# Attention into a two-layer MLP on one core: loads and weights in a new order, the fifth unit's attention outputs beside the output product, DVE's normalising tiles first

## The chip, the cores and the metric

The kernel runs on one core of one Trainium2 chip. The metric is the device time of one execution in microseconds (us); smaller is better. The engines of the core work side by side and wait for each other by semaphores: PE (TensorE, matrix products, with PEld for its weight loads), ACT (ScalarE), DVE (VectorE), POOL (GpSimd) and SP (SyncE, which here only issues DMAs).

## The reference, cut to what matters

```python
# q, k, v: (8 batches, 12 heads, 448 rows, 64), times 0.1
scores = matmul(q, k.T) / sqrt(64)
m = max(scores, axis=-1)
e = exp(scores - m)
attn = e / (sum(e, axis=-1) + exp(-m) + 1e-9)
x = concat_heads(matmul(attn, v))          # (8 * 448, 768)
h = x @ w_in                               # w_in  (768, 2048)
g = h * tanh(softplus(h))                  # Mish
out = g @ w_out                            # w_out (2048, 768)
```

Inputs and output are float32; the kernel casts to bfloat16 for its matrix products.

## The kernel before, in words

**Pairs and units.** Two heads are a pair: 48 pairs, p = 0 to 47, six to a batch. Three pairs are a unit u; two units are a batch. The first six pairs (u = 0 and 1) run in a loop of their own, the head. From u = 2 on, one iteration of the main loop does two parts. The attention part has twelve steps, n = 0 to 11, four for each of the unit's three pairs. The matrix part, f = 0 to 7, multiplies the attention output of the batch two units back by an eighth of `w_in` at a time. The third to sixth unit of the title are u = 2 to 5, and the fifth is u = 4.

**A step of attention.** `scores` writes one score tile (PE) and takes its row maxima (DVE, line 293). There are three score tiles of two banks each, and `scores_ahead` keeps up to three filled. `exps` takes the exponentials on ACT (line 306); after it the tile is free. Of a pair's four steps three have two column blocks, and one has one block and leaves its second bank unused.

**Normalising.** `normalise(p)` multiplies the seven column blocks of a pair's exponentials (the buffer `en`) by the reciprocal denominators `rden`. In the head POOL does four (`shared=4`) and DVE three (lines 339 and 341); POOL reads its own copy of the reciprocals (line 331). In later units DVE does two pairs and POOL the third (`on_pool`). The result is turned either by a DMA transpose on SP's queue (line 345) into `eT`, or on PE by `turn_on_pe` (line 356) for the pairs in `BY_PE` (2, 4, 5, 6, 7).

**Attention output.** `av_pair` does eight matmuls (line 382) from `eT` and `v_bf` and copies the result into `xT` (line 391). It writes either one of the two product tiles `mo` (`mo_take`), or, where `bank` is given, the unused second bank of a pair's last score tile. The main loop uses the second way for all units from u = 4 on, through `av_with`. For u = 2 and 3 the list `AV_AT` says after which step which pair's output is made in a product tile.

**The products.** `mm1_mish` does the first product and Mish (lines 406 and 412). `mm2_part` does the second (line 472) for 128 rows and a number of quarters of the 768 columns; `plan` says which parts belong to which unit. A part is cut into chunks of two matmuls, which the attention steps take in between as filler, by `weight`. `gather_mid` copies 64 rows of each of two batches into one tile, used by the part with i = 3. Copies out of the product tiles are put off (`late`) until the next `flush_late`.

**Loads.** `load_pair` issues the three loads of a pair (224 KB each) on SP's queue, where the DMA transposes and the stores of the output stand too, each in the order of the program. `cast_pair` casts them on POOL. In the main loop both happen at the steps n = 0, 3 and 6 (`LOAD_AT`): loads four pairs ahead, casts three. `load_w` issues the twenty pieces of the weights (twelve of `w_in` with 256 KB, eight of `w_out` with 384 KB) on POOL's queue, by `W_HEAD` in the head and by `W_AT` from u = 2 to 4, with two more at f = 2 and 6 of u = 2.

What the engines do is in the order of the program; there is no scheduler behind it (`manual_schedule`).

Of the kernel before, what the change touches and what calls it, by code (L numbers as in the profile page):

```python
# [9 lines left out]
FP32 = mybir.dt.float32  # L10
BF16 = mybir.dt.bfloat16
AF = mybir.ActivationFunctionType
ALU = mybir.AluOpType
# [6 lines left out]
def kernel(  # L20
# [9 lines left out]
    nc = tc.nc  # L30
# [6 lines left out]
    SP_ = S // NT  # L37
# [3 lines left out]
    NTILE = 2 * S // 128  # L41
    UNITS_PER_B = HP // UNIT_PAIRS
# [10 lines left out]
    def pool(name, bufs, space=None):  # L53
        if space is None:
            return ctx.enter_context(tc.tile_pool(name=name, bufs=bufs))
        return ctx.enter_context(tc.tile_pool(name=name, bufs=bufs, space=space))
# [6 lines left out]
    st_pool = pool("st", 5)  # L63
# [48 lines left out]
    def flush_late():  # L112
        while late:
            late.popleft()()
# [8 lines left out]
    def load_pair(p, which="qkv"):  # L123
        if p >= N_PAIRS:
            return
        b, h0 = p // HP, (p % HP) * 2
        tiles = loaded.setdefault(p, [])
        for nm, src in (("q", q), ("k", k), ("v", v)):
            if nm not in which:
                continue  # L130
            t = ld_pool.tile([SP_, 2, NT * D], FP32, tag=f"{nm}_f", name=f"{nm}_f")
            nc.sync.dma_start(
                out=t, in_=src[b, h0 : h0 + 2].rearrange("h (p t) d -> p h (t d)", t=NT)
            )
            tiles.append(t)
# [19 lines left out]
    def load_w(n):  # L155
        for _ in range(min(n, len(pieces))):
            dst, src = pieces.popleft()
            nc.gpsimd.dma_start(out=dst, in_=src.rearrange("(a p) c -> p a c", p=128))
# [80 lines left out]
    def scores_ahead(limit):  # L239

        while rg["next"] < limit and rg["used"] < len(sc_tiles):
            rg["used"] += 1
            scores(rg["next"])
            rg["next"] += 1
# [80 lines left out]
    def normalise(p, dma=True, on_pool=False, shared=0):  # L325
        st = att[p]
        en = st["en"]
        if on_pool or shared:

            st["rden2"] = st_pool.tile([128, NTILE], FP32, tag="rden2", name="rden2")  # L330
            nc.vector.tensor_copy(out=st["rden2"], in_=st["rden"])  # L331
        for i in range(NTILE):
            pool_does = on_pool or i < shared
            args = dict(
                out=en[:, :, i, 0:SP_], in0=en[:, :, i, 0:SP_],
                scalar1=st["rden2" if pool_does else "rden"][:, i : i + 1],
            )
            if pool_does:
                nc.gpsimd.tensor_scalar(scalar2=1.0, op0=ALU.mult, op1=ALU.mult, **args)  # L339
            else:  # L340
                nc.vector.tensor_scalar(scalar2=None, op0=ALU.mult, **args)  # L341
        eT = eT_pool.tile([128, NT, 2 * S], BF16, tag="eT", name="eT")
        st["eT"] = eT
        if dma:
            nc.sync.dma_start_transpose(
                out=eT.rearrange("c j (i q) -> c (j i) q", q=128),
                in_=en.rearrange("q j i c -> q (j i c)"),
            )
# [64 lines left out]
        if not spare:  # L413
            mo_free.append(h_ps)

    def gather_mid(b):

        g, half = divmod(b, 2)
        if half == 0:
            mids[g] = mid_pool.tile([128, FF_T, 128], BF16, tag="mid", name="mid")  # L420
        at = S - 64 if half == 0 else 0
        nc.vector.tensor_copy(
            out=mids[g][:, :, 64 * half : 64 * half + 64], in_=gT[b][:, :, at : at + 64]
        )

# [59 lines left out]
    first_mm2 = 2 * UNITS_PER_B  # L485

    def whole(g, i):
        return [(g, i, 0, 2), (g, i, 2, 2)]
# [3 lines left out]
    plan = {}  # L492
    for g in range(B // 2):
        u0 = first_mm2 + 4 * g
        rest = plan.pop(u0, [])
        if g == 0:
            plan[u0] = [(0, i, 0, 2) for i in range(2)] + [(0, 2, 0, 1)]
            plan[u0 + 1] = [(0, 2, 1, 1)] + [(0, i, 2, 2) for i in range(3)]
        else:
            plan[u0] = rest + whole(g, 0) + [(g, 1, 0, 1)]  # L500
            plan[u0 + 1] = [(g, 1, 1, 1), (g, 1, 2, 2)] + whole(g, 2)
        plan[u0 + 2] = [(g, 4, 0, 2), (g, 4, 2, 1)] + whole(g, 3)
        plan[u0 + 3] = [(g, 4, 3, 1)] + whole(g, 5) + [(g, 6, 0, 2)]
        if g < B // 2 - 1:
            plan[u0 + 4] = [(g, 6, 2, 2)]
        else:
            plan[u0 + 3] += [(g, 6, 2, 1), (g, 6, 3, 1)]
# [4 lines left out]
    BY_POOL = 4  # L512
    LEAD = UNIT_PAIRS + 1
    LOAD_AT = (0, 3, 6)
    LAST_AV_AT = (0, 6, 9)
    HEAD = HP

# [9 lines left out]
    }  # L527
    AV_HEAD = {(3, 3): 0, (4, 2): 2, (4, 3): 1}
    W_HEAD = {0: 3, 1: 1, 3: 1, 4: 1}
    AV_AT = ({3: 4, 7: 3, 9: 5}, {5: 6, 8: 7, 10: 8})  # L530

    W_AT = ({5: 1, 9: 1}, {1: 1, 4: 1, 5: 1, 7: 1, 9: 1, 11: 1}, {3: 1, 5: 1, 7: 1, 9: 1})
    for which in ("qk", "v"):
        for p in range(UNIT_PAIRS):
            load_pair(p, which)
# [39 lines left out]
    for u in range(UNITS_PER_B, N_UNITS + 2 * UNITS_PER_B):  # L575
        attn = u < N_UNITS
        filler = deque()
        for part in plan.get(u, []):
            filler.extend(mm2_part(*part))
        total, done, acc = sum(w for _, w in filler), 0, 0.0  # L580
        p0 = u * UNIT_PAIRS
        if attn and u >= first_mm2:
            av_with.update({p0 + i: p0 + i - UNIT_PAIRS for i in range(UNIT_PAIRS)})
        end = min((u + 1) * UNIT_PAIRS, N_PAIRS) * STEPS

        for n in range(steps):
            pi, s = divmod(n, STEPS)
            p, idx = p0 + pi, p0 * STEPS + n
            late_tp = u == UNITS_PER_B and n == STEPS
            if late_tp:  # L590
                transpose_pair(p0 + 2)
            exps(idx)
            if late_tp:
                evac_qk(p0 + 2)
            if u == UNITS_PER_B + 1:
                for part in TURN_AT[1].get(n, []):
                    turn_on_pe(*part)
            flush_late()
            acc += weight[n]
            want = int(total * acc / sum(weight) + 1e-6)  # L600
            while done < want:
                fn, w = filler.popleft()
                fn()
                done += w
            scores_ahead(end)
            if n in LOAD_AT:
                load_pair(p0 + LOAD_AT.index(n) + LEAD)
                cast_pair(p0 + LOAD_AT.index(n) + LEAD - 1)
            if u - UNITS_PER_B < len(AV_AT):
                early = AV_AT[u - UNITS_PER_B]  # L610
                if n in early:
                    av_pair(early[n])
                if u == UNITS_PER_B:
                    for part in TURN_AT[0].get(n, []):
                        turn_on_pe(*part)
            elif u == N_UNITS and n in LAST_AV_AT:
                av_pair(p0 - UNIT_PAIRS + LAST_AV_AT.index(n))
            if u - UNITS_PER_B < len(W_AT):
                load_w(W_AT[u - UNITS_PER_B].get(n, 0))
        assert done == total  # L620

        moe = u < N_UNITS + UNITS_PER_B
        b, w = (u - UNITS_PER_B) // UNITS_PER_B, u % UNITS_PER_B
        nxt = p0 + UNIT_PAIRS
        todo = sorted(range(p0, nxt), key=lambda p: p in BY_PE)
        for f in range(FF_U):
            if moe:
                mm1_mish(b, w * FF_U + f)
            if u == UNITS_PER_B and f in (2, 6):
                load_w(1)  # L630
            if not attn:
                continue
            if f == 0:
                denominators(att[p0]["whole"])
                normalise(todo[0], dma=todo[0] not in BY_PE)
            if f in (1, 3, 5):
                transpose_pair(nxt + f // 2, bank=f // 2 % 2)
                evac_qk(nxt + f // 2)
            if nxt < DIAG_FROM and f in (4, 6):
                scores_ahead(nxt * STEPS + f // 2 - 1)  # L640
            if f == FF_U - 1:
                scores_ahead(min(nxt * STEPS + 3, N_PAIRS * STEPS))
            if f == 3:
                normalise(todo[1], dma=todo[1] not in BY_PE)
            if f == 4:
                normalise(todo[2], dma=todo[2] not in BY_PE, on_pool=True)
        if attn and u + 1 < N_UNITS:

            nc.scalar.activation(out=one, in_=zero, func=AF.Exp)
        if moe and w == UNITS_PER_B - 1:  # L650
            gather_mid(b)
    flush_late()
    assert not pieces and all(have == 4 for _, have in o_sbs.values())
# [30 lines left out]
```

## Time and profile before

| | us |
|---|---|
| median of 3 runs | 480.37 (480.23 to 481.23) |
| profiled execution, its own time | 479.95 |
| its span, first to last instruction | 478.0 |
| busy: PE | 443.1 (93%) |
| busy: ACT | 350.0 (73%) |
| busy: DVE | 339.1 (71%) |
| busy: POOL | 181.1 (38%) |
| moved by DMA | 90.37 MB, mean 189 GB/s |

The mean granted clock of PE was 0.982. In the lines of the profile, a row of a timeline has the start and the duration in us, the engine, the line of the kernel, the operation with output and inputs, the count of instructions that were merged into the row, and in brackets the idle time of the engine before it and what ended that. A row of the chain of waits has start, duration and what was being done. `SPq` is the queue of DMAs that SP issues. Slices are fortieths of the span, 11.95 us each.

### The profile page before, as it was taken

Reading aid. Unit: us, or ns where it says so; the run is one execution under the profiler, and the core shown is the slowest. Engines: PE = TensorE matmul, PEld = TensorE weight load, DVE = VectorE, ACT = ScalarE, POOL = GpSimd, SP = SyncE. Lnnn points to the kernel's source line nnn. Section 1 sums busy time; section 2 is a strip of 40 time slices with the busy share of each in tenths; the row PEclk is TensorE's granted clock in tenths of the full one; section 3 lists DMA queues with packets and bytes.
Section 4 is the critical chain, followed back from the end, with each engine's and each line's share of the span. In section 5 each row is a group of like instructions: output and inputs, shape, how many; then the busy total and the mean of one; then the engine's idle time right before and its main releaser. Section 6 shows DMA issues by size and latency. Waiting matters only on the chain.

```text
span 478.0 us, 8924 instructions
## 1 busy us (share of the span) xinstructions
PE 443.1 (93%) x3064; PEld 248.6 (52%) x3064; DVE 339.1 (71%) x680; ACT 350.0 (73%) x919; POOL 181.1 (38%) x315
## 2 busy tenths in 40 slices
PE   4565888898999999999999999999999999999997
PEld 2233544454655555555555555556555555556565
DVE  4888987968787886878687878788787869420021
ACT  5979678878787888979787878888897978412300
POOL 4877809255514334353535242433535340300000
PEclk9998798899999999999999999999999999999999
DMA  8999969999999989899999999899989595870113
GB/s 228 220 233 220 235 100 234 162 187 238 207 217 276 206 212 219 213 203 246 193 250 182 225 167 228 211 207 234 201 233 212 156 178 127 135 164 24 43 28 105
DMA packets 202381, 90.37 MB, mean 189 GB/s; under 512 B 159072, under 2 KB 198880, under 8 KB 202336
## 3 DMA queue, kind: packets, MB, share of 16 engines
q1 hardware_dynamic: 194848, 83.51, 81.3%
q0 software_dynamic: 7488, 6.29, 8.6%
q8 instruction: 24, 0.39, 0.3%
q14 instruction: 21, 0.17, 0.1%
HBM read 45.61 MB, written 11.01 MB: 118 GB/s over the span
## 4 chain that ended last, share of the span: by engine, by line
PE 76%; ACT 10%; DVE 9%; issue 2%; DMA 1%; POOL 0%; SPq 0%; DVEq 0%; ACTq 0%; POOLq 0%
PE mo L472 26%; PE mo L406 25%; ACT en L306 9%; PE sc L382 6%; DVE negm L293 6%; PE sc L266 5%; PE sc L406 4%; PE sc L193 3%; PE sc L272 2%; PE mo L356 1%; PE mo L382 1%; DVE en L341 1%; PE sc L280 1%; DVE eT L360 1%; DMA k_f<-in_k_dram 1%
## 5 line engine op out<-in xcount | busy, mean ns | idle before, releaser
L306 ACT ACTIVATE en<-sc,negm 128x448 bf16<-128x448 f32 x336 | 209.6, 637 | 26.4 <-DVE xT L391 10.4
L293 DVE TENSOR_REDUCE negm<-sc 128x2 f32<-128x896 f32 x192 | 180.7, 968 | 55.8 <-PE sc L275 26.0
L472 PE MATMUL mo<-w_out_sb,gT 128*128 128x384 bf16 (+1 forms) x912 | 142.3, 301 | 0.0
L406 PE MATMUL mo<-xT,w_in_sb 128*128 128x448 bf16 x672 | 137.7, 353 | 0.6 <-DVE xT L391 0.6
L412 ACT ACTIVATE gT<-mo 128x448 bf16<-128x448 f32 x112 | 61.3, 547 | 68.2 <-PE mo L406 68.1
L472 PEld LDWEIGHTS <-gT 128*128 128x128 bf16 x912 | 84.1, 98 | 48.2 <-issue 5.7
L339 POOL TENSOR_SCALAR en<-en,rden 128x448 bf16<-128x448 bf16 x122 | 76.4, 646 | 80.7 <-DVE rden L331 76.9
L406 PEld LDWEIGHTS <-w_in_sb 128*128 128x128 bf16 x768 | 72.9, 98 | 64.0 <-issue 3.0
L306 ACT ACTIVATION_READ_ACCUMULATOR en<-sc,negm 128x1 f32 x336 | 69.3, 206 | 0.0
L175 POOL CAST q_bf<-q_f 112x512 bf16<-112x512 f32 x47 | 29.0, 617 | 98.4 <-DMA q_f<-in_q_dram 98.0
L341 DVE TENSOR_SCALAR en<-en,rden 128x448 bf16<-128x448 bf16 x214 | 58.6, 345 | 0.9
L459 DVE COPY o_sb<-mo 128x384 f32<-128x384 f32 (+1 forms) x65 | 32.2, 495 | 35.1 <-PE mo L472 34.8
L266 PE MATMUL sc<-kT,qd 128*128 128x448 bf16 x168 | 47.7, 354 | 0.3 <-ACT en L306 0.2
L272 PE MATMUL sc<-kT,qd 64*128 64x448 bf16 x72 | 25.1, 411 | 12.7 <-ACT en L306 11.1
L382 PE MATMUL sc<-eT,v_bf 112*64 112x448 bf16 x288 | 34.1, 357 | 1.9 <-ACT en L306 1.7
L162 POOL CAST v_bf<-v_f 112x512 bf16<-112x512 f32 x48 | 29.5, 616 | 9.7 <-DMA v_f<-in_v_dram 8.8
L382 PEld LDWEIGHTS <-v_bf 112*64 112x64 bf16 x384 | 21.0, 112 | 22.8 <-issue 13.6
L176 POOL CAST k_bf<-k_f 112x512 bf16<-112x512 f32 x47 | 28.9, 616 | 7.5 <-DMA k_f<-in_k_dram 7.0
L227 DVE TENSOR_SCALAR qd<-sc 64x448 bf16<-64x448 bf16 x48 | 18.7, 389 | 11.9 <-PE sc L193 11.2
L266 PEld LDWEIGHTS <-qd 128*128 128x128 bf16 x168 | 16.3, 97 | 18.0 <-issue 9.2
L275 PE MATMUL sc<-kT,qd 64*128 64x448 bf16 x72 | 25.4, 415 | 0.0
L472 PE MATMUL mo<-w_out_sb,mid 128*128 128x384 bf16 x128 | 24.9, 326 | 0.0
(57 smaller groups left out, 340.1 us busy)
## 6 DMA issues: line engine op xcount, KB each, us to landing
q_f<-in_q_dram SPq DMA_DIRECT2D x48, 224.0 KB, 5.1
k_f<-in_k_dram SPq DMA_DIRECT2D x48, 224.0 KB, 5.4
v_f<-in_v_dram SPq DMA_DIRECT2D x48, 224.0 KB, 5.7
w_in_sb<-in_moe_w_in_dram POOLq DMA_DIRECT2D x12, 256.0 KB, 6.1
w_out_sb<-in_moe_w_out_dram POOLq DMA_DIRECT2D x8, 384.0 KB, 7.6
out_dram<-o_sb SPq DMA_DIRECT2D x7, 336.0 KB, 3.3
out_dram<-o_sb SPq DMA_DIRECT2D x8, 288.0 KB, 4.6
out_dram<-o_sb SPq DMA_DIRECT2D x8, 240.0 KB, 2.9
```

What stands on the lines that cost most here:

```text
L162: nc.gpsimd.tensor_copy(out=casted[p][2], in_=loaded.pop(p)[2])
L266: nc.tensor.matmul(sc[:, bk, 0:S], lhsT=qT[:, i].rearrange("d h r -> d (h r)"), rhs=kT, start=True, stop=True,)
L272: nc.tensor.matmul(sc[:, 0, 0:S], lhsT=qT[0:64, qa : qa + 128], rhs=kA, start=True, stop=True)
L293: nc.vector.tensor_reduce(out=negm, in_=sc[:, 0 : len(cols), 0:S], axis=AX.X, op=ALU.max, negate=True)
L306: nc.scalar.activation(out=st["en"][:, :, c, 0:SP_], in_=sc[:, bk, 0:S].rearrange("q (j c) -> q j c", j=NT), func=AF.Exp, bias=st["negm"][ ...
L339: nc.gpsimd.tensor_scalar(scalar2=1.0, op0=ALU.mult, op1=ALU.mult, **args)
L341: nc.vector.tensor_scalar(scalar2=None, op0=ALU.mult, **args)
L382: nc.tensor.matmul(av[h * 64 : (h + 1) * 64, 0:S], lhsT=v_bf[:, h, j * D : (j + 1) * D], rhs=e_h, start=(j == 0), stop=(j == NT - 1),)
L406: nc.tensor.matmul(h_ps[:, 0:S], lhsT=w_in_sb[:, dm, ff * 128 : (ff + 1) * 128], rhs=xT[b][:, dm, :], start=(dm == 0), stop=(dm == DM_T - 1),)
L412: nc.scalar.activation(out=gT[b][:, ff, :], in_=h_ps[:, 0:S], func=AF.Mish)
L459: nc.vector.tensor_copy(out=o_sb[:, cols], in_=st["o"][:, 0:n_cols])
L472: nc.tensor.matmul(st["o"][:, 0:n_cols], lhsT=src[:, ff, c0 : c0 + 128], rhs=w_out_sb[:, ff, cols], start=(ff == 0), stop=(ff == FF_T - 1),)
```

## The change

Four things are changed.

- `normalise`: DVE's tiles are issued first, then the copy of the reciprocals, then POOL's tiles. Before, the copy came first and POOL's tiles stood ahead of DVE's in the program.
- The loads of u = 2 to 4 follow a table: pair 13 is loaded at n = 9 and pair 14 at f = 1 of u = 2; pair 15 at n = 0 and pair 16 at f = 5 of u = 3; pair 17 at n = 0 and pair 18 at f = 1 of u = 4. Casts stay where they were. The weight pieces of u = 2 to 4 move by some steps: both of the matrix part of u = 2 at f = 2; in u = 3 one from n = 11 to n = 2; in u = 4 two each at n = 1 and n = 4, before one each at 3, 5, 7 and 9.
- In u = 4 the attention outputs of pairs 9, 10 and 11 are made in product tiles after the steps 2, 7 and 9, and no more in the score tiles. The copy of `gather_mid(0)` moves from DVE, at the end of u = 3, to POOL, after step 7 of u = 4.
- The second product has six quarters in u = 4 and six in u = 5, before five and seven; the part of 128 rows that was cut into two single quarters stays whole.

```diff
     def normalise(p, dma=True, on_pool=False, shared=0):
         st = att[p]
         en = st["en"]
-        if on_pool or shared:
-
-            st["rden2"] = st_pool.tile([128, NTILE], FP32, tag="rden2", name="rden2")
-            nc.vector.tensor_copy(out=st["rden2"], in_=st["rden"])
-        for i in range(NTILE):
-            pool_does = on_pool or i < shared
-            args = dict(
-                out=en[:, :, i, 0:SP_], in0=en[:, :, i, 0:SP_],
-                scalar1=st["rden2" if pool_does else "rden"][:, i : i + 1],
-            )
-            if pool_does:
-                nc.gpsimd.tensor_scalar(scalar2=1.0, op0=ALU.mult, op1=ALU.mult, **args)
-            else:
-                nc.vector.tensor_scalar(scalar2=None, op0=ALU.mult, **args)
+        n_pool = NTILE if on_pool else shared
+
+        def scaled(i, rden):
+            tile_i = en[:, :, i, 0:SP_]
+            return dict(out=tile_i, in0=tile_i, scalar1=rden[:, i : i + 1])
+
+        for i in range(n_pool, NTILE):
+            nc.vector.tensor_scalar(scalar2=None, op0=ALU.mult, **scaled(i, st["rden"]))
+        if n_pool:
+
+            rden2 = st_pool.tile([128, NTILE], FP32, tag="rden2", name="rden2")
+            nc.vector.tensor_copy(out=rden2, in_=st["rden"])
+            for i in range(n_pool):
+                nc.gpsimd.tensor_scalar(
+                    scalar2=1.0, op0=ALU.mult, op1=ALU.mult, **scaled(i, rden2)
+                )
...
-    def gather_mid(b):
+    def gather_mid(b, copy=nc.vector.tensor_copy):
...
-        nc.vector.tensor_copy(
+        copy(
...
         if g == 0:
-            plan[u0] = [(0, i, 0, 2) for i in range(2)] + [(0, 2, 0, 1)]
-            plan[u0 + 1] = [(0, 2, 1, 1)] + [(0, i, 2, 2) for i in range(3)]
+            plan[u0] = [(0, i, 0, 2) for i in range(3)]
+            plan[u0 + 1] = [(0, i, 2, 2) for i in range(3)]
...
+    LOADS = {
+        2: ({0: 10, 3: 11, 6: 12, 9: 13}, {1: 14}),
+        3: ({0: 15}, {5: 16}),
+        4: ({0: 17}, {1: 18}),
+    }
...
-    AV_AT = ({3: 4, 7: 3, 9: 5}, {5: 6, 8: 7, 10: 8})
-
-    W_AT = ({5: 1, 9: 1}, {1: 1, 4: 1, 5: 1, 7: 1, 9: 1, 11: 1}, {3: 1, 5: 1, 7: 1, 9: 1})
+    AV_AT = ({3: 4, 7: 3, 9: 5}, {5: 6, 8: 7, 10: 8}, {2: 9, 7: 10, 9: 11})
+
+    W_AT = ({5: 1, 9: 1}, {1: 1, 2: 1, 4: 1, 5: 1, 7: 1, 9: 1}, {1: 2, 4: 2})
...
-        if attn and u >= first_mm2:
+        if attn and u > first_mm2:
             av_with.update({p0 + i: p0 + i - UNIT_PAIRS for i in range(UNIT_PAIRS)})
...
+            if u in LOADS:
+                if n in LOADS[u][0]:
+                    load_pair(LOADS[u][0][n])
+            elif n in LOAD_AT:
+                load_pair(p0 + LOAD_AT.index(n) + LEAD)
             if n in LOAD_AT:
-                load_pair(p0 + LOAD_AT.index(n) + LEAD)
                 cast_pair(p0 + LOAD_AT.index(n) + LEAD - 1)
...
+            if (u, n) == (first_mm2, 7):
+                gather_mid(0, nc.gpsimd.tensor_copy)
...
-            if u == UNITS_PER_B and f in (2, 6):
-                load_w(1)
+            if u == UNITS_PER_B and f == 2:
+                load_w(2)
+            if u in LOADS and f in LOADS[u][1]:
+                load_pair(LOADS[u][1][f])
...
-        if moe and w == UNITS_PER_B - 1:
+        if moe and w == UNITS_PER_B - 1 and b > 0:
             gather_mid(b)
```

## The prediction

> **What bounds the kernel now.** I read the page's slices first, then the chain of waits, then the timelines of the engines over the stretch that the diff touches (0 to 160 us).
>
> ```profile
> PE   4565888898999999999999999999999999999997
> PEclk9998798899999999999999999999999999999999
> DMA  8999969999999989899999999899989595870113
> ```
>
> TensorE (PE) is full from the tenth slice on, so whatever the early units win or lose is carried to the end unchanged. The DMA engines are nearly full too, with a hole only in the sixth slice (60 to 72 us). A unit from u=6 on lasts 26.0 us (154.84 to 180.83). Unit u=4 lasts 25.9 (102.2 to 128.1), u=5 26.7 (128.1 to 154.84). The PE timeline of these two:
>
> ```profile
> 105.67 0.95 PE L382 MATMUL sc<-eT,v_bf 112*64 112x448 bf16 x8 [0.32 <-ACT en L306]
> ...
> 111.06 0.95 PE L382 MATMUL sc<-eT,v_bf 112*64 112x448 bf16 x8 [0.83 <-ACT en L306]
> ...
> 115.99 0.95 PE L382 MATMUL sc<-eT,v_bf 112*64 112x448 bf16 x8 [0.52 <-ACT en L306]
> ...
> 117.73 1.30 PE L406 MATMUL mo<-xT,w_in_sb 128*128 128x448 bf16 x6
> ...
> 143.81 1.30 PE L406 MATMUL mo<-xT,w_in_sb 128*128 128x448 bf16 x6
> ...
> 149.41 0.36 PE L193 MATMUL sc<-ident,q_bf 112*128 112x112 bf16 x4 [0.51 <-DVE qd L214]
> ```
>
> In u=4 PE idles before each attention output (L382), since that writes a score tile which ACT's exponentials must first leave; with 0.21 at 114.44 that is 1.88 us. Its attention part lasts 14.84 (102.89 to 117.73) with five output quarters, that of u=5 15.04 (128.77 to 143.81) with seven and no idle time. ACT and DVE there:
>
> ```profile
> 109.67 0.63 ACT L306 ACTIVATE en<-sc,negm 128x448 bf16<-128x448 f32 x1 [0.68 <-DVE negm L293]
> ```
>
> ```profile
> 17.36 0.82 DVE L341 TENSOR_SCALAR en<-en,rden 128x448 bf16<-128x448 bf16 x3
> ...
> 28.85 1.13 DVE L341 TENSOR_SCALAR en<-en,rden 128x448 bf16<-128x448 bf16 x3
> ...
> 108.55 3.08 DVE L293 TENSOR_REDUCE negm<-sc 128x2 f32<-128x896 f32 x3
> ...
> 120.00 1.81 DVE L341 TENSOR_SCALAR en<-en,rden 128x448 bf16<-128x448 bf16 x7
> ...
> 146.09 2.97 DVE L341 TENSOR_SCALAR en<-en,rden 128x448 bf16<-128x448 bf16 x7
> ```
>
> DVE's seven normalising tiles take 1.81 us alone and 2.97 at 146.09, where POOL casts; in the head three take 0.82 or, beside POOL's four, 1.13. POOL:
>
> ```profile
> 29.11 2.60 POOL L339 TENSOR_SCALAR en<-en,rden 128x448 bf16<-128x448 bf16 x4 [1.47 <-DVE rden L331]
> ...
> 146.66 0.73 POOL L175 CAST q_bf<-q_f 112x512 bf16<-112x512 f32 x1 [2.40 <-DMA q_f<-in_q_dram]
> ```
>
> The head, in the chain of waits and in ACT's timeline:
>
> ```profile
> 31.45 0.98 PE mo L356 x7
> ...
> 33.85 1.11 PE mo L382 x8
> ```
>
> ```profile
> 35.01 0.53 ACT L391 CAST xT<-mo 128x448 bf16<-128x448 f32 x1 [2.21 <-PE mo L382]
> ```
>
> PE turns pair 2's seven tiles right behind POOL, then does pair 0's attention output, and ACT idles 2.21 us for it: this stretch sets the pace. SP's queue:
>
> ```profile
> 95.03 13.69 SPq L345 DMA_TRANSPOSE eT<-en  x3
> ...
> 121.87 16.58 SPq L345 DMA_TRANSPOSE eT<-en  x3
> ...
> 138.50 0.57 SPq L132 DMA_DIRECT2D q_f<-in_q_dram  x1
> ```
>
> A DMA transpose (0.92 MB) holds SP for 4.3 us alone; u=4's three took 7.2, 4.2 and 4.9, the first beside the last weight pieces (issued until 119.8). All loads of u=5 wait behind them.
>
> **The change part by part**, against the profiled execution's 479.95 (span 478.0 and 1.95 around it; 0.42 under the median 480.37).
>
> *DVE's tiles first* (head, pairs 0 to 5). POOL now starts behind DVE's three tiles: 0.82 less the 0.08 that the copy of the reciprocals took in the queue, +0.74. Its four tiles then run alone: 0.62 each as in the rows of seven (4.33), 2.50 for 2.60. POOL ends 0.64 later; its casts follow, with a pair's slack. Pair 2: PE reaches POOL's fourth tile at 31.39 + 3 x 0.13 = 31.78, POOL ended at 31.71 and will end at 32.35: +0.57, straight into ACT's 2.21. Pair 4 (POOL 43.84 + 2.60, PE at 46.30): fourth tile at 46.69, POOL at 47.08, +0.39, of which the 0.19 between PE's end (47.29) and DVE's pick-up (47.48) is free: +0.20. Pair 5's tiles are on DVE's own chain at 49.83: 1.13 becomes 0.82, -0.31. Pairs 0, 1, 3 go by DMA and are used many us later (20.48 for 33.78): nothing. Sum **+0.46**; bounds -0.31 (POOL never waited for) and +0.96.
>
> *Attention outputs of pairs 9 to 11 in u=4.* They leave the score tiles for the two product tiles, behind steps 2, 7 and 9. Each product tile is free by then (its copy ran a step earlier), and their eT landed by 111 (104.5 + 6.2). Eight matmuls stay eight, but PE no longer waits for ACT before them and the single-column reduction no longer stands behind 0.95 us of them. The copies of xT move too: DVE's reduction of 108.55 was late behind one and an output copy, ACT's idle 0.68. PE without its idle time: 14.84 - 1.88 = 12.96, plus a sixth quarter (8 x 0.163 = 1.31): 14.27. Following steps with ACT at 0.61 per exponential leaves about 0.1: 14.4, **-0.45**. Bounds -0.57 and +0.5 (an output copy of 0.55 waited for).
>
> *Six quarters in u=5.* A quarter less on PE (-1.31) meets ACT: u=4 with five quarters and this form of attention output took 14.84. Here the first output copy is made before the fourth score tile and not between two reductions (0.46 less on DVE). Followed step by step it comes to 14.5, by the row of u=4 to 14.84; I take 14.64, nearer to the first, **-0.40**; bounds -0.1 and -1.31. Two 192-wide halves become one 384-wide: 32 x 0.082 against 16 x 0.163, nothing.
>
> *gather_mid(0) on POOL.* DVE loses 0.78 at 105.63, where it then idled 0.60 for PE: nothing there. POOL's 1024 elements are not in the trace; by casts of 512 at 0.56 apart, 1.1 us, from 0.78 (DVE's) to 1.4 (0.62 per 448). Its user is in u=6; behind it on POOL wait only the copies of q_rest (122.17), idle until then for DVE. What it collides with is a rival.
>
> *Loads and weights.* Load 13 goes into the DMA hole, 14 and 15 two us earlier: their casts (77 to 83 us) never waited, so nothing. Third-unit weight piece ten: 60 us for 76.5, used at 97, nothing. In u=4 weight pieces 16 and 17 go out at 106 and not 115, 18 and 19 behind cast 16 (which waits for its load), by 118. First use of them is at once in u=5, 128.7 for 132.2; a piece lands in 7.6, so 126. POOL's queue behind cast 16 holds only cast 17 and the copy. On SP load 18 stands between u=4's first and second transpose: 1.5 us of issue and up to 3.0 of DMA (0.67 MB at 220 GB/s). The first transpose should fall from 7.2 to 4.4, so the second starts at 128.1 against 129.2 and, sharing the DMA, lands near 136; its attention output comes at 136.3. Third: lands 140.6 for 141.4. I put **+0.20**, bounds 0 and +2.1.
>
> *u=5's matrix part.* It lasted 11.03 (143.81 to 154.84) against 10.37 in u=4: 0.66 lost where cast 20 (load late, behind the transposes) ran into DVE's tiles. SP now stores the first output tile before load 19, load 20 leaves at about 140.8 (141.1 before) and lands at 146, DVE's tiles start at 145.4 (146.09): they overlap for 1.1 us, not 2.0. **-0.40**; bounds 0 and -0.66.
>
> Sum: +0.46 - 0.45 - 0.40 - 0.40 + 0.20 = **-0.59**: 479.36 for the profiled execution, **479.8** for the median.
>
> **The rivals.** 0.2% is 0.96 us, about what a measurement of this kernel can tell from no change: faster is under 479.4, slower over 481.3.
>
> *POOL's later start is not felt* (ACT or the turning PE has slack that the rows hide): the head gives -0.31 and not +0.46, the rest holds, 0.77 less: 479.0. For it: PE's seven turned tiles took 1.05 against 0.99 elsewhere, so POOL was only just felt. Against: PE ran without a gap from 30.90 to 35. Chance 0.24.
>
> *The late second transpose* (slower). If the first transpose still takes 7.2, it ends at 129.1, load 18 at 130.6, the second transpose at 136.3 and lands at 138.4, against 136.3 wanted: PE waits 2.1, ACT behind it. No gain in u=5's matrix part: 480.37 + 0.46 - 0.45 - 0.40 + 2.1 = 482.1. It decides once the first transpose ends after 127. For it: DMA is at 200 to 215 GB/s from 118 to 126. Against: half of those weights go 9 us earlier. Chance 0.18.
>
> *ACT bounds both units*: u=4 gains 0.2, u=5 0.1, the collision stays: 480.37 + 0.46 - 0.30 = 480.5. For it: 21 exponentials and two table loads are most of 15 us; against: the 1.4 us that ACT idles in u=4. Chance 0.12.
>
> *The copy on POOL meets DVE's tiles in u=4* (cast 17 and the copy, 118.9 to 121.7, on DVE's 119.5). At the measured 1.16 per 2.03 us of casts, 2.3 us of POOL cost DVE 1.3; PE's slack there was 0.56 (122.11 to 122.67) and grows by 0.5: +0.3, 480.1; if DVE waits out all of POOL's time, +1.3, 481.1. Chance 0.10. The Trainium skill (SBUF — State Buffer, section "SBUF: two separate sides") says that the pair of ports which DVE's fast modes share with GpSimd is held for a whole instruction and the other side fully blocks. By that rule the higher of the two prices holds; the 2.97 us agree in direction, but 1.16 is less than the casts' whole time.
>
> **How the numbers follow.** Forecast 0.36, its own range 479.2 to 480.4. Faster: 0.23 of the first rival and 0.13 of the forecast, 0.36. Slower: 0.17 of the late transpose and 0.03 of the copy's tail, 0.20. The rest, 0.44, lies within. The range from 478.6 to 481.6 leaves out both gains at their bounds and the upper part of the late transpose.
>
> **What would show it.** Head: POOL's tiles start 0.7 later, three DVE tiles take 0.8, ACT's idle before the first xT copy grows from 2.21 to 2.8. u=4: no idle before L382, attention part 14.4. u=5: 14.6, and its normalising tiles under 2.97. First transpose of u=4 near 4.4. I am wrong if the matrix part of u=4 starts no earlier relative to its table load, if L382 in u=5 waits for a DMA, or if the head does not shift.

## The result and the profile after

The changed kernel takes 483.27 us in the median (482.89 to 483.73) against 480.3 for the kernel before beside it: ratio 1.0062, 95% interval 1.0039 to 1.0086, so 3.0 us slower (1.9 to 4.1). The forecast was 479.8, with a range up to 481.6. The profiled execution spans 481.9 us, 3.9 more than that of before, at the same mean granted clock of 0.982.

The slices of the page:

```profile
PE   4576798799889999999999999999999999999997
PEclk9998798999989999999999999999999999999999
DMA  8999999899999989899999999898989695770103
```

The hole of the DMA engines in the sixth slice is filled, as meant. But PE now has 8s in the eleventh and twelfth slices (120 to 145 us), and the granted clock an 8 in the twelfth, where all were 9 before. I cut the run at the starts of the matrix parts and took each length in both traces. The head is 0.64 longer, u=3 0.87 shorter (before, the granted clock was 0.50 there from 89 to 92; no other kernel's trace here has such a stretch at that place), u=4's attention part 0.54 longer (15.45 to 15.99 between two matrix parts), u=4's matrix part 1.65 longer (10.43 to 12.08), u=5's attention part 2.58 longer (15.65 to 18.23) and u=5's matrix part 0.67 shorter (11.10 to 10.43). From u=6 on the two are equal. The sum is +3.87.

PE's timeline, with the waits of u=4 and u=5 in the brackets:

```profile
106.64 0.54 PE L266 MATMUL sc<-kT,qd 128*128 128x448 bf16 x2 [0.39 <-DVE negm L293]
...
113.05 0.54 PE L266 MATMUL sc<-kT,qd 128*128 128x448 bf16 x2 [0.43 <-ACT en L306]
...
118.04 1.30 PE L408 MATMUL mo<-xT,w_in_sb 128*128 128x448 bf16 x6 [0.29 <-DVE xT L393]
...
124.62 0.36 PE L193 MATMUL sc<-ident,q_bf 112*128 112x112 bf16 x4 [1.48 <-DVE qd L214]
...
140.09 1.43 PE L384 MATMUL sc<-eT,v_bf 112*64 112x448 bf16 x8 [2.02 <-DMA eT<-en]
```

The first three are u=4's attention part: no wait before an attention output (L382 before, L384 now), but other waits in their place. The fourth is in u=4's matrix part and new. The fifth is pair 13's output in u=5; after this wait the granted clock falls to 0.61 and 0.54 for two stretches of 2 us, and the eight matmuls take 1.43 for 0.95. An attention output of u=5 that waits for a DMA is one of the signs that the prediction names for being wrong.

DVE's seven normalising tiles in u=4, first the row of the timeline and then the answer for that line (minimum, median and maximum of one tile in ns), and in u=5:

```profile
118.90 5.37 DVE L335 TENSOR_SCALAR en<-en,rden 128x448 bf16<-128x448 bf16 x7
...
150.63 2.29 DVE L335 TENSOR_SCALAR en<-en,rden 128x448 bf16<-128x448 bf16 x7
```

```profile
L335 DVE TENSOR_SCALAR en<-en,rden x7: 322/681/2220, 118.9 to 123.9; 128x448 bf16<-128x448 bf16 x7
```

Before, the seven of u=4 took 1.81. What POOL did then:

```profile
105.80 1.55 POOL L158 DMA_DIRECT2D w_out_sb<-in_moe_w_out_dram  x2
116.26 0.61 POOL L175 CAST q_bf<-q_f 112x512 bf16<-112x512 f32 x1 [8.91 <-DMA q_f<-in_q_dram]
...
118.84 0.61 POOL L162 CAST v_bf<-v_f 112x512 bf16<-112x512 f32 x1 [0.39 <-DMA v_f<-in_v_dram]
119.39 1.48 POOL L158 DMA_DIRECT2D w_out_sb<-in_moe_w_out_dram  x2
120.86 0.63 POOL L175 CAST q_bf<-q_f 112x512 bf16<-112x512 f32 x1
...
122.61 1.03 POOL L424 COPY mid<-gT 128x1024 bf16<-128x1024 bf16 x1
```

POOL waits 8.91 us for load 16 (5.93 before), and then everything behind it comes in one block from 118.84 to 123.64: the last cast of pair 16, two weight pieces, pair 17, the copy. DVE's tiles, 118.90 to 124.27, run beside that block from its start to its end. SP's queue:

```profile
124.34 4.98 SPq L347 DMA_TRANSPOSE eT<-en  x1
...
131.06 10.52 SPq L347 DMA_TRANSPOSE eT<-en  x2
```

The first transpose of u=4 needs those tiles. It is shorter than before (4.98 for 7.2) but starts 2.5 us later; load 18 follows, and the second transpose starts at 131.06, where the forecast had 128.1. PE's wait of 2.02 is for that one.

### The profile page after: what moved, and what is told of

The parts are those of the page before. It is cut to its first block, busy times and chain, and to the rows that moved or that the text cites. A ratio compares the mean times of both kernels' runs of the same rounds, so it can differ in the third digit from the quotient of the medians.

```text
span 481.9 us, 8886 instructions
## 1 busy us (share of the span) xinstructions
PE 445.6 (92%) x3048; PEld 247.8 (51%) x3048; DVE 341.1 (71%) x678; ACT 349.3 (72%) x919; POOL 180.7 (37%) x316
## 4 chain that ended last, share of the span: by engine, by line
PE 77%; DVE 9%; ACT 7%; DMA 4%; issue 2%; SPq 1%; POOL 1%; DVEq 0%; ACTq 0%; POOLq 0%
PE mo L408 26%; PE mo L474 26%; PE sc L384 6%; ACT en L306 6%; PE sc L266 6%; DVE negm L293 5%; PE sc L408 4%; PE sc L193 3%; PE sc L272 2%; DMA eT<-en 2%; PE mo L384 2%; DVE eT L362 1%; DMA q_f<-in_q_dram 1%; DVE en L335 1%; PE mo L358 1%
## 5 line engine op out<-in xcount | busy, mean ns | idle before, releaser
L474 PEld LDWEIGHTS <-gT 128*128 128x128 bf16 x896 | 82.9, 98 | 50.2 <-issue 7.8
L341 POOL TENSOR_SCALAR en<-en,rden 128x448 bf16<-128x448 bf16 x122 | 75.3, 635 | 79.1 <-DVE rden L339 70.8
L335 DVE TENSOR_SCALAR en<-en,rden 128x448 bf16<-128x448 bf16 x214 | 60.5, 353 | 1.1
L384 PE MATMUL sc<-eT,v_bf 112*64 112x448 bf16 x264 | 31.7, 361 | 2.5 <-DMA eT<-en 2.0
L384 PEld LDWEIGHTS <-v_bf 112*64 112x64 bf16 x384 | 20.0, 110 | 23.1 <-issue 10.9
```

The lines of the kernel that those rows point to most:

```text
L335: nc.vector.tensor_scalar(scalar2=None, op0=ALU.mult, **scaled(i, st["rden"]))
L384: nc.tensor.matmul(av[h * 64 : (h + 1) * 64, 0:S], lhsT=v_bf[:, h, j * D : (j + 1) * D], rhs=e_h, start=(j == 0), stop=(j == NT - 1),)
L474: nc.tensor.matmul(st["o"][:, 0:n_cols], lhsT=src[:, ff, c0 : c0 + 128], rhs=w_out_sb[:, ff, cols], start=(ff == 0), stop=(ff == FF_T - 1),)
```

## The experiments

Each is a few lines of one of the two kernels. "Part" means the time between two matrix parts unless it says matrix part. The diffs are cut to the lines that say what changed.

**The loads and weights alone.** Before, with only the change's lists:

```diff
+    LOADS = {2: ({0: 10, 3: 11, 6: 12, 9: 13}, {1: 14}),
+             3: ({0: 15}, {5: 16}), 4: ({0: 17}, {1: 18})}
-    W_AT = ({5: 1, 9: 1}, {1: 1, 4: 1, 5: 1, 7: 1, 9: 1, 11: 1}, {3: 1, 5: 1, 7: 1, 9: 1})
+    W_AT = ({5: 1, 9: 1}, {1: 1, 2: 1, 4: 1, 5: 1, 7: 1, 9: 1}, {1: 2, 4: 2})
-            if u == UNITS_PER_B and f in (2, 6):
-                load_w(1)
+            if u == UNITS_PER_B and f == 2:
+                load_w(2)
```

> The kernel before with only the change's table of loads and its weight steps: normalising, quarters, attention outputs and the copy on DVE stay as before. Theory (these lists alone make late loads and transposes): cast 16 waits over 8 us for its load, DVE's seven tiles of u=4 take 3 to 5 us, the second transpose lands after PE wants it, PE waits 1 to 2.5 us for a DMA in u=5: 481.4 to 483. Rival (the collision needs the copy on POOL too): tiles under 2.2, no PE wait, 480.0 to 480.8.

Measured: 482.01 us, ratio 1.0038 (1.0023 to 1.0054), +1.8 us. As the theory has it: cast 16 waits 8.85 us, PE waits 1.25 in u=4's matrix part (11.85 long) and 1.07 before pair 13's output in u=5 (the row names DVE; the second transpose ended at 134.85, and the output starts 9.1 us after that transpose began, in the changed kernel 9.0). The tiles of u=4:

```profile
118.84 3.73 DVE L341 TENSOR_SCALAR en<-en,rden 128x448 bf16<-128x448 bf16 x7
```

So the lists alone make DVE meet POOL; the copy only lengthens it.

**Which of the lists.** The changed kernel with only u=4's weight pieces back at 3, 5, 7 and 9:

```diff
-    W_AT = (..., {1: 2, 4: 2})
+    W_AT = (..., {3: 1, 5: 1, 7: 1, 9: 1})
```

> The changed kernel, with only the weight pieces of the fifth unit (u=4) put back to steps 3, 5, 7 and 9. Theory (the early weight pieces 16 and 17 stand in front of load 16 on the DMA engines, cast 16 comes four us late, and POOL's casts, weights and copy then all meet DVE's normalising tiles): cast 16 starts near 112.5 and not 116.3; the seven tiles take 2.5 to 3.5 us and not 5.37; the wait of PE for them falls from 1.48 to under 0.7, the wait of pair 13's attention output for its DMA transpose from 2.02 to under 1; time 480.6 to 481.6, some 2 us under the changed kernel's 483.3. Rival (the copy on POOL alone is to blame): the tiles still take about 5, nothing gained, 483. Rival (load 18 between the transposes alone is to blame for the DMA wait): PE's 1.48 goes, the 2.02 stays; 481.8.

Measured: 483.77 us, 1.0068 (1.0042 to 1.0093), missed by 2 us and more. One half came out: cast 16 starts at 113.99, 3.26 after SP issued its load (7.16 in the changed kernel, behind the two weight pieces of 105.80), the tiles take 2.10, u=4's matrix part 10.44 with no wait. But now four weight pieces (1.57 MB) go out between 116.6 and 122.3, the first transpose takes 7.44 and the second starts at 132.58:

```profile
141.26 0.95 PE L384 MATMUL sc<-eT,v_bf 112*64 112x448 bf16 x8 [3.25 <-DMA eT<-en]
```

The early weight pieces thus do two things: they delay load 16 by 3.9 us, and they shorten the first transpose, since only two pieces are left beside it. With two late pieces it took 4.89 to 5.67 in eight kernels, with four 6.26 to 9.03 in six (before: 7.21).

The copy on POOL is not free here either: it runs from 119.80 to 120.84, and DVE's denominators, 0.18 us before, take 0.94 beside it, although the tiles behind them no longer meet it.

```profile
119.95 0.94 DVE L319 SCALAR_TENSOR_TENSOR den<-sums,expm 128x21 f32<-128x21 f32 x1
```

**Load 18 out of the transposes' way.**

```diff
-        4: ({0: 17}, {1: 18}),
+        4: ({0: 17, 3: 18}, {}),
```

> The changed kernel, with load 18 issued right behind load 17 (after step 3 of u=4) and so ahead of the unit's first transpose, as before the change. Theory (DVE's late tiles delay the first transpose by 2.5 us, and load 18 the second by 1.7 more): the tiles stay at about 5.4 and PE's 1.48 stays, but the second transpose lands 2 us earlier, its wait of 2.02 shrinks to 0 to 0.5 and the slow clock behind it goes; time 480.8 to 481.8. Rival (the late tiles alone delay the transposes): the wait stays at 1.5 or more, 483.

Measured: 482.03 us, 1.0025 (1.0010 to 1.0041). PE's wait for the DMA in u=5 is gone and the part is 15.68; the tiles (5.09) and PE's wait in u=4 (1.42) stay. The time is 0.2 above what was expected. In u=5 PE now waits for ACT before two outputs:

```profile
139.47 0.95 PE L384 MATMUL sc<-eT,v_bf 112*64 112x448 bf16 x8 [0.60 <-ACT en L306]
...
144.86 0.95 PE L384 MATMUL sc<-eT,v_bf 112*64 112x448 bf16 x8 [0.74 <-ACT en L306]
```

Together 1.34, and the quarter taken off u=5 was 1.31 of PE: it became idle time, and the part is as long as with seven quarters (15.65).

**Both of these edits at once.**

> The changed kernel with two edits undone at once: the weight pieces of u=4 at the steps 3, 5, 7 and 9 as before, and load 18 at n=3 of u=4 so that it does not stand between the first and the second DMA transpose. Theory (the loss in u=4 and u=5 is two queue collisions, each removed by one of the edits): no PE wait for qd in u=4's matrix part, part about 10.4; no DMA wait in u=5, its attention part 15.6 to 15.8; what stays is the head and u=4's sixth quarter (+0.55): 481.0 to 481.6. Rival (the first transpose runs beside the last weight pieces whatever load 18 does, 7.4 us): the second one lands about 1 us late, PE waits that long in u=5: 482.2 to 482.8. Second rival (the loss sits elsewhere, in the head or the attention parts): 483 as after.

Measured: 482.06 us, 1.0036 (1.0019 to 1.0053). The theory is wrong here and the rival's mechanism right, at a little less than its time: no wait in u=4's matrix part (10.44), but the first transpose takes 7.81 beside the four late pieces, with load 18 nowhere near, and PE waits 1.44 for the second.

**The copy back on DVE.** The changed kernel with `gather_mid(0)` as before:

```diff
-            if (u, n) == (first_mm2, 7):
-                gather_mid(0, nc.gpsimd.tensor_copy)
-        if moe and w == UNITS_PER_B - 1 and b > 0:
+        if moe and w == UNITS_PER_B - 1:
```

> The changed kernel, with only the copy of gather_mid(0) back on DVE at the end of u=3. Theory (the casts and weights that came late are most of POOL's time beside DVE's tiles; the copy is the last 1.03 us of it): the seven tiles take 4.2 to 4.5 instead of 5.37, PE's wait falls from 1.48 to about 0.4, the first transpose of u=4 starts 1 us earlier and the wait for the second falls from 2.02 to about 1; time 481.6 to 482.4. Rival (the copy alone is to blame): the tiles take 1.8 to 2, no wait of PE, 480.5.

Measured: 482.93 us, 1.0046 (1.0027 to 1.0066), above what was expected, and not to be told from the changed kernel by its interval. In its trace (of an execution of 481.57, under that median) the tiles take 3.76 for 5.37, u=4's matrix part is 10.47 without a wait, the second transpose starts at 129.90, and PE still waits 1.71 for it.

**The order in `normalise`.** Once undone in the changed kernel, once done alone in the kernel before (the first hunk of the diff).

> The changed kernel, with only normalise in its old order (copy of the reciprocals first, POOL's tiles beside DVE's). Theory: the head is 0.64 us longer in the changed kernel (first product at 64.04 against 63.40), and this order is all of it: the first product starts at 63.3 to 63.6, and the rest is as in the changed kernel; time 482.5 to 483. Rival (the order saves DVE time and the head's loss has another cause): the first product at 64.0 or later, 483.3 or more.

> The kernel before with only the new order in normalise: DVE's tiles, then the copy of the reciprocals, then POOL's tiles. Theory of the prediction (POOL starts 0.7 later, PE reaches its fourth tile too early): ACT idles about 3.3 before the first xT copy, the first product starts 0.5 to 1.0 later than before on the same chip: 480.9 to 481.4. Rival (the start of the first product varies by as much from one execution to the next, and the order itself is not felt): 480.2 to 480.6.

Measured: undone, 482.28 us, 1.0041 (1.0024 to 1.0058), 1.0 under the changed kernel's median and 0.2 under the theory's range, though the two were not timed side by side. Its trace does not show that gain: the profiled execution was the slowest of its eight (485.63), and its first product starts at 65.43, not at 63.6 or earlier. Alone, 481.61 us, 1.0029 (1.0015 to 1.0043): +1.4 us (0.7 to 2.1), above the theory's range. An execution's first exponential starts anywhere from 7.5 to 8.3 us, so I count from there. The first `xT` copy then starts at 28.06 to 28.09 in all six kernels with the new order, and at 26.95 to 27.48 in seven of the eight with the old one (27.85 in norm_before, which had lost 0.4 in an earlier step). In ACT's timeline of the changed kernel, and in PE's just before:

```profile
35.66 0.53 ACT L393 CAST xT<-mo 128x448 bf16<-128x448 f32 x1 [3.34 <-PE mo L384]
```

```profile
31.89 0.68 PE L358 MATMUL mo<-ident,en 128*112 128x128 bf16 x4 [0.26 <-POOL en L341]
```

With the wait of 0.26 and the three tiles before it, PE's seven turned tiles of pair 2 last 1.69 (30.88 to 32.57) for 1.05 before: that is the 0.6 which the prediction has for pair 2. In the first `xT` copy the new order lies 0.6 behind the median of those seven, 27.44. The first product starts at 56.45 to 57.43 with the new order (median 57.13) and at 55.34 to 56.42 in those seven (55.84); norm_before has 57.32. In four of the six the further 0.65 or more came after pair 2; in b_norm it lies in pair 5's block. The windows of b_norm and of before there (length, PE busy, matmuls, granted clock, DMA share, GB/s):

```profile
58.00:59.00 1.00, 1.00 (x8) 0.50 1.06 254
```

```profile
58.00:59.00 1.00, 1.00 (x13) 1.00 1.13 200
```

Matmuls of pair 5 ran there at half the granted clock. Where that stretch falls differs between executions of the old order too (f1 has it at 56 to 60), so that the order moves it is not shown.

**The attention outputs and the quarters.** The kernel before with the outputs of pairs 9 to 11 in product tiles, and then with six quarters in both units besides:

```diff
-    AV_AT = ({3: 4, 7: 3, 9: 5}, {5: 6, 8: 7, 10: 8})
+    AV_AT = ({3: 4, 7: 3, 9: 5}, {5: 6, 8: 7, 10: 8}, {2: 9, 7: 10, 9: 11})
-        if attn and u >= first_mm2:
+        if attn and u > first_mm2:
```

> The kernel before with only the attention outputs of pairs 9, 10 and 11 in product tiles, five quarters in u=4 and seven in u=5. Theory of the prediction: no PE wait of 0.3 or more before an attention output of u=4, its attention part (15.45 between the matrix parts) 14.9 to 15.0, u=5 unchanged at 15.65: 479.6 to 480.0. Rival (the gain goes into waits for product tiles): 15.3 to 15.7, 480.1 to 480.5.

> The kernel before with the attention outputs of pairs 9, 10 and 11 in product tiles and six quarters in u=4 and in u=5. Prediction: u=4 15.0 and u=5 15.25 between the matrix parts (0.45 and 0.40 less), 479.3 to 479.7. Theory after the result (a sixth quarter costs its 1.31 on PE in u=4 less what the product tiles win, and u=5 is held by ACT so that a quarter less wins nothing): 15.9 to 16.1 and 15.6 to 15.7, 480.6 to 481.1.

Measured: product tiles alone 480.85 us, 1.0021 (1.0000 to 1.0041), above both sides of its expectation; with six quarters 481.37 us, 1.0025 (1.0012 to 1.0037), 0.3 above the second theory's range. u=4's part grew from 15.45 to 16.45 with the product tiles, a thing that neither side of the first expectation reached. PE's timeline of b_av:

```profile
114.45 0.95 PE L382 MATMUL mo<-eT,v_bf 112*64 112x448 bf16 x8 [1.10 <-DVE o_sb L459]
```

The output waits for a product tile that DVE has not emptied: that copy started at 113.85, behind a reduction that had itself waited for ACT. With six quarters the part is 16.00, 0.45 less than with five, although it does more; the quarters then end at other steps. u=5's part is 15.70 with six quarters, as the second theory has it. These two parts are 0.6 of the 1.2 us that this edit costs in the median; where the rest lies the trace does not show.

**A version that is faster than both.** Load 16 right behind load 15, in front of u=3's transposes, in the kernel before:

```diff
+    LOADS = {2: ({0: 10, 3: 11, 6: 12, 9: 13}, {1: 14}),
+             3: ({0: 15, 3: 16}, {}), 4: ({0: 17, 3: 18}, {})}
```

> The kernel before with a new order of loads alone: 13 at n=9 and 14 at f=1 of u=2, 15 and 16 at n=0 and n=3 of u=3, 17 and 18 at n=0 and n=3 of u=4; weights, normalising, quarters and attention outputs as before. Theory (load 16 came late behind u=3's three transposes, and all that stands behind cast 16 on POOL with it): cast 16 waits under 1 us for its load, the weight pieces of u=4 are issued by 116, the first transpose of u=4 takes under 5 us, loads 19 and 20 leave SP earlier, u=5's normalising tiles take under 2.3 and its matrix part 10.4: 479.4 to 480.0. Rival (the first transpose's 7.2 is not due to the weights, or u=5's collision stays): 480.2 to 480.6, no change.

Measured: 479.66 us, 0.9994 (0.9982 to 1.0006), no difference that can be told. Cast 16 no longer waits, u=4's three transposes take 14.42 together (16.58 before), the first 5.11 (7.21), a little over the 5 of the theory, although the last two weight pieces still go out at 118.07 and not by 116; u=5's tiles take 1.81 and its matrix part 10.44. But u=4's part went from 15.45 to 16.39. Pair 16's casts now follow pair 15's at once (105.61 to 107.34), and DVE's copy meets them, 2.43 us for 0.78:

```profile
105.18 2.43 DVE L422 COPY mid<-gT 128x1024 bf16<-128x1024 bf16 x1
```

So I moved that copy to POOL, but behind n=4, where POOL is free:

```diff
+            if (u, n) == (first_mm2, 4):
+                gather_mid(0, nc.gpsimd.tensor_copy)
```

> The kernel f1 (before with the earlier loads) with the copy of gather_mid(0) moved from DVE to POOL behind step n=4 of u=4, where POOL has nothing else to do for 5 us. In f1 this copy met the three casts of pair 16 and took 2.43 us on DVE for 0.78, and u=4's attention part grew by 0.94 (15.45 to 16.39). Theory (the copy's wait for POOL is that loss, and DVE's reductions from PSUM are not held by POOL): DVE goes on with its reduction at once, attention part of u=4 15.4 to 15.5, DVE's tiles of u=4 and u=5 stay at 1.8, median 478.4 to 479.1. Rival (the reductions or the single-column one are late for another reason): part 16.0 or more, 479.5 as f1.

Measured: 478.93 us, 0.9975 (0.9962 to 0.9988), 1.2 us faster than before and within the theory's range. u=4's part is 15.44. POOL's copy and, beside it, DVE's three reductions, at 1.03 each as elsewhere:

```profile
107.95 1.05 POOL L422 COPY mid<-gT 128x1024 bf16<-128x1024 bf16 x1
```

```profile
107.96 3.08 DVE L293 TENSOR_REDUCE negm<-sc 128x2 f32<-128x896 f32 x3
```

With the product tiles for pairs 9 to 11 added to it:

> The kernel f3 with, besides, the change's attention outputs of pairs 9, 10 and 11 in product tiles behind steps 2, 7 and 9 of u=4, five quarters there and seven in u=5 as before. Theory of the prediction (PE no longer waits for ACT before these outputs): attention part of u=4 0.4 to 0.6 shorter than in f3, 14.9 to 15.0, median 478.0 to 478.5. Rival (in the product tiles the outputs wait for the output copies, and nothing is won): as f3 or up to 0.3 slower.

Measured: 479.91 us, 0.9992 (0.9981 to 1.0003): the gain is lost again, by more than the rival had. u=4's part is 16.44, with the same 1.10 behind an output copy.

## Why the prediction was wrong, step by step

*DVE's tiles first* (+0.46): the mechanism was right, the size too small. POOL's tiles start 0.72 later counted from the first exponential (29.36 less 7.59 against 29.11 less 8.06), and pair 2 costs 0.6 as worked out (0.57). Pair 4 costs more than its 0.20: PE waits 0.25 at 47.75, and from pair 4's denominators to the copy of its first turned half it is 4.75 for 4.21 to 4.41 in those seven kernels, 0.3 to 0.5. Pair 5's gain is there: from its denominators to the copy behind DVE's tiles it is 1.24 (50.03 to 51.27) for 1.62 (49.01 to 50.63). Together that is 0.6 to 0.8. Alone the edit costs 1.4 in the median (0.7 to 2.1). A half-clock stretch adds 0.65 or more in four of the six profiled executions with the new order, and in one of those seven with the old; whether the order brings it is open. The rival "not felt" is out.

*Attention outputs in u=4* (-0.45): the term that failed is the 0.1 left for idle time. PE's own work was right: 14.27 without idle time. But the three waits shown above make 1.11: 0.39 for a reduction, 0.43 for an exponential and 0.29 for the copy of pair 11's output. 14.27 and 1.11 make 15.38, and PE took 15.39, from 102.65 to 118.04, where the forecast had 14.4. The premise that "each product tile is free by then (its copy ran a step earlier)" held in the changed kernel, where no output waits for its tile. With five quarters it failed (b_av, f4_copy_av): the copy was late behind a reduction, and the output of pair 10 waited 1.10, twice the 0.55 of the prediction's bound.

*Six quarters in u=5* (-0.40): nothing, 15.68 and 15.70 for 15.65. I had taken the value between a step-by-step count and the nearest row and leant to the count. The rival that ACT bounds the unit was right there.

*The copy on POOL* (nothing) and *loads and weights* (+0.20, bounds 0 and +2.1) failed together. I treated load 16 as unmoved. In fact the early weight pieces, issued at 105.80, held it up: cast 16 starts 7.16 us after the load's issue, for 3.29 before and 3.26 with these pieces back in their old place (w4_before). I then wrote that POOL's queue behind cast 16 holds "only cast 17 and the copy", as a count of instructions; what mattered was that all of them run when cast 16 is let go, which is when DVE's tiles come. The rival of the copy had the place right, and its higher price was still too low: the tiles lost 3.56 us, 1.92 by the casts and the weight pieces (b_loads_w; an issue of two weight pieces beside the tiles accounts for 0.2 to 0.3, by the 2.02 and 2.10 of b_six_av and w4_before) and 1.6 more by the copy (5.37 less gather_dve's 3.76). By the Trainium skill (SBUF — State Buffer, section "SBUF: two separate sides") the port pair is held for a whole instruction and the other side fully blocks. The trace agrees and goes further: one tile of 0.33 us took 2.22, longer than any single POOL instruction there.

The rival of the *late second transpose* came true by another road. I had tied it to a first transpose of 7.2 us. It took 4.98, but began 2.5 us later because its input, DVE's tiles, was late. Late tiles alone do not make PE wait: with load 18 out of the way the wait is gone though the tiles take 5.09 (load18_early), and without the copy PE still waits 1.71 (gather_dve). Load 18 between the transposes is thus part of the road; whether it would do with timely tiles and two late weight pieces was not run. I had given this rival and that of the copy chances of their own, 0.18 and 0.10, though the late load 16 feeds both.

*u=5's matrix part* (-0.40): 0.67 in the end, but by luck. Load 20 left 3.2 later than before (144.30 for 141.09) and not 0.3 earlier; the tiles met less of its casts because they came 4.5 later (150.63 for 146.09), behind the 2.58 that u=5 had lost. In load18_early, where that loss is gone, the part is 11.05 for 11.10.

Done alone, the normalising order, the lists, and the outputs with the quarters cost 1.4, 1.8 and 1.2 us; that is 4.4, against 3.0 for the whole change. Each interval is 0.6 to 0.8 wide on either side, so I read no more into the difference.

## What to carry to other kernels

Before a DMA is moved earlier, list what it now stands ahead of in the shared engines, and follow the one that is pushed back to the engine that waits for it: the instructions queued behind that wait come out as one block, and the question is what they meet. A copy given to another engine is free only at a time when the engine that it shares a path with has no work of the kind that collides; here the same copy cost 1.6 us of DVE's time behind n=7 when load 16 was late, 0.8 behind n=7 when it was not (w4_before), and nothing behind n=4. Rivals that share a cause should be priced as one chain.

## What the hardware showed that I had not expected

- DVE's normalising tiles (bfloat16, SBUF to SBUF) are held through several POOL instructions in a row, 2.22 us for one of 0.33, and its 0.78 copy became 2.43 beside casts. Its reductions of score tiles ran at 1.03 beside the same POOL copy.
- A DMA transpose of 0.92 MB took 4.9 to 5.7 us with two weight pieces issued in the 5 us before it (eight kernels) and 6.3 to 9.0 with four in the 8 us before it (six kernels).
- After a wait of PE of 2.02 us the granted clock was 0.61 and 0.54 over the next 4 us, and part of the loss in u=5 (0.48 on one group of eight matmuls) is that. In norm_before it was 0.50 from 143 to 146, after a wait of 2.10. But it stayed at 1.00 after 3.25 in w4_before and after 1.71 in gather_dve, so that the wait causes it is not shown.
